# The out-projection as seven block products (Strassen's scheme) instead of eight, in a fused attention and gated-MLP kernel

## The chip, the cores and the metric

The kernel runs on one core of a Trainium2 chip. The metric is the device time of one execution in microseconds; the time of the kernel before is the median of three executions. A profile of one further execution gives the span of the program and what every engine did in it. The engines are called PE (TensorE, matmuls; PEld is its weight load), DVE (VectorE), ACT (ScalarE), POOL (GpSimd) and SP (SyncE, which issues the DMAs).

## The reference

```python
def _attn_ref(q, k, v):                      # q, k, v: 8 x 8 x 576 x 64
    scores = (1 / np.sqrt(D)) * np.matmul(q, k.transpose(0, 1, 3, 2))
    rel = pos[:, None] - pos[None, :]
    mask_local = (rel >= 0) & (rel < 32)                         # heads 0 to 3
    mask_strided = (rel >= 0) & (pos[None, :] % 32 == pos[:, None] % 32)  # heads 4 to 7
    ...
    return np.matmul(softmax(scores), v)

def _moe_ref(x, w_in, w_spatial, b_spatial, w_out):   # x: 8 x 576 x 512
    h = np.maximum(x @ w_in, 0.0)                      # 512 -> 1024
    u, v = h[..., :512], h[..., 512:]
    v_n = (v - mean(v)) / np.sqrt(var(v) + 1e-06)
    v_s = np.einsum('ts,bsd->btd', w_spatial, v_n) + b_spatial[None, :, None]
    gated = u * v_s
    return gated @ w_out                               # 512 -> 512
```

The result of the attention, with its heads side by side, is the x of the second function. All of it is float32.

## The kernel before, in words

The work goes batch by batch (eight batches of 576 positions). Attention makes x in pieces, a pair of heads at a time, two batches ahead of the matrix stages where it can; its matmuls are small. Then each batch has four matrix stages, all on PE:

- `moe_1` computes the v half of h in tiles of 128 positions by 512 columns (L874), which ACT moves out of PSUM with the ReLU and DVE normalises, and the u half transposed, in tiles of 128 features by 288 positions (L916).
- `moe_tail` does the last 64 positions of the normalisation, for one batch (batches 0 and 1) or for two together (the later ones).
- `moe_2` does the spatial matmul for one half of the positions at a time (288 of them; four tiles of 128 features each, L997, L1009, L1010), and DVE multiplies each tile into u (L1019). Then comes the out-projection of that half (`project`, L1039): four tiles of 128 output columns by 288 positions, each a sum over four blocks of 128 features. So the order in a batch is spatial of half 0, project of half 0, spatial of half 1, project of half 1.

PE multiplies float32 numbers in a rounded format here. To keep the accuracy, both operands of every large product are split into a high part (rounded: `rnd`, on ACT, DVE or POOL, L372 and L374) and a remainder (`rest`, a subtraction on DVE, L382), and three products are summed (`PROD`): high by high, high by remainder, remainder by high. A project of one half thus takes 4 tiles x 4 blocks x 3 = 48 matmuls of 288 columns, and a batch takes 96. `gated` is split tile by tile into two buffers of the ring `g`; the weight w_out is split once, at the start, into `w_out_sb` (`weight`, `weights`). ACT copies each finished tile of the output from PSUM to a buffer of the ring `o` (`evac`, L394), and a DMA stores it.

Buffers come from rings: u, g, vv, o and s (PSUM) have two buffers each, vn has one, and the matmul tiles `m` have four PSUM banks. A buffer is written again only when its last reader is done.

No engine chooses at run time. `Program.order()` simulates the program once with a table of priorities (`KEYS`), costs for each engine and latencies, and emits for each engine one fixed sequence; an instruction that waits holds up everything behind it on its engine. The simulation also puts filler matmuls on zeros (L1172) where PE would idle early on; they keep its clock up. `weights` loads each quarter of w_in and w_out (8 bytes a word, packed) into stage buffers of vn, u and g, rebuilds the numbers on ACT, POOL (L758) and DVE (L766), and splits them.

Of the kernel before, what the change touches and what calls it, by code (L numbers as in the profile page):

```python
# [9 lines left out]
F32 = mybir.dt.float32  # L10
F32R = mybir.dt.float32r
# [29 lines left out]
    "a": (-825.9, -1662.1, -696.1, -506.6, 76.7, 35.0, 162.7, 122.5,),  # L41
    "v": (-216.6, -1140.4, -156.0, 19.8,),
    "u": (-158.4, -165.3, 0.3, 367.0,),
    "s": (2476.0, -453.8, 2782.5, 3198.4,),
    "t": (2534.3,),
    "o": (641.4, -137.9, 1268.2, 1486.2,),
    "cst": (-2628.8,),
    "lead": (-0.22,),
    "fill": (170.7, 2011.8, -4312.7, 693.0, -265.9, 735.5,),
    "dp": (844, -15182,),  # L50
    "dpt": (83.09,),
    "lv": (-430.1, -2526.4, -200.5, -140.6,),
    "lu": (-99.7, -488.1, -137.6, -250.6,),
    "lo": (435.1, 82.8, -874.1, 81.6,),
    "ls": (781.6, 39.6, 3113.7, 831.6, 1021.7,),
    "near": (122.22,),
# [6 lines left out]
PROD = ((0, 0), (0, 1), (1, 0))  # L63
FLAT = {2: "p n -> p n", 3: "p a b -> p (a b)", 4: "p a b c -> p (a b c)"}
# [249 lines left out]
def attention_moe(ctx, tc, qT, kT, vl, vs, cst, eye, w_in, w_out, wsp, wtail, out):  # L314
# [14 lines left out]
    w_out_sb = sb.tile([P, 2, NT, DM], F32R, name="w_out_sb")  # L329
# [26 lines left out]
    r_o = Ring(sb, "o", [P, HS], F32, 2)  # L356
# [370 lines left out]

    def weight(key, fetch, src, n, dst, tok, stage):

        buf, i = stage
        if src.dtype == F32:
            val = lambda: buf().bitcast(F32).rearrange(FLAT[len(buf.ring.shape)])[:, 2 * i * n : 2 * i * n + n]
            load(fetch, val, src, [(buf, i, 0), (buf, i, 1)], P * n * 4)
        else:
            raw = lambda dt: buf().bitcast(F32).rearrange(FLAT[len(buf.ring.shape)])[  # L740
                :, 2 * i * n : 2 * (i + 1) * n
            ].bitcast(dt)
            half = lambda j, dt=I32: raw(dt).rearrange("p (n t) -> p n t", t=2)[:, :, j]
            low, top = (buf, i, 0), (buf, i, 1)
            val = lambda dt=F32: half(1, dt)
            load(fetch, lambda: raw(I32), src.bitcast(I32), [low, top], P * n * 8)

            add(
                key, [(ACT, 110 + 0.87 * n)],
                lambda eng: eng.activation(val(), val(), AF.Prelu, scale=2.0**-112, alpha=2.0**32),  # L750
                [], [top],
            )
            def lowest(eng):
                if hasattr(eng, "bn_stats"):
                    eng.tensor_scalar(half(0), half(0), 29, None, op0=ALU.logical_shift_right)
                else:
                    byte = raw(U8).rearrange("p (n t) -> p n t", t=8)[:, :, 3]
                    eng.tensor_scalar(half(0), byte, 1 / 32, -15.5 / 32, op0=ALU.mult, op1=ALU.add)  # L758

            add(  # L760
                key, [(DVE, 70 + 0.52 * n), (POOL, 110 + 1.8 * n)], lowest,
                [], [low], port=(DVE,),
            )
            add(
                key, [(DVE, 70 + 1.04 * n)],
                lambda eng: eng.scalar_tensor_tensor(  # L766
                    half(1), half(1), 3, half(0),
                    op0=ALU.logical_shift_left, op1=ALU.bitwise_or,
                ),
                [low], [top], port=(DVE,),  # L770
            )
# [4 lines left out]
    def weights():  # L776
# [14 lines left out]
        for n, job in enumerate(jobs):  # L791

            def put(job=job, n=n):
                stage = (first, n) if n < NT else ((r_g if n % 2 else r_u).new(), 0)
                weight(*job, stage)
# [457 lines left out]
```

## Time and profile before

| | us |
|---|---|
| median of three executions | 525.32 (524.07, 525.76, 525.32) |
| span of the profiled execution | 521.6 |
| PE busy in that span | 508.8 |
| DVE busy | 332.9 |
| ACT busy | 229.1 |
| POOL busy | 83.6 |

The page gives no time of the profiled execution apart from its span. The 3.7 us by which the median is longer lie around the span, and they are taken to be the same for both kernels.

In the rows of the profile a group reads: line, engine, operation, what it writes <- what it reads, shape, count, then busy time, mean duration in ns, and the idle time of the engine just ahead of these instructions with what ended it. A row of the timeline starts with the start in us and the duration in us; "x6" is that many instructions in a row, and the bracket holds the idle time ahead. A row of the windows gives busy time in us and instructions for PE, PEld, DVE, ACT and POOL, then the granted clock of PE as a share of full speed, the busy share of the DMA engines, and GB/s.

### The profile page before, as it was taken

The numbers are of one execution on the slowest core, as the hardware profiler recorded it, in microseconds if no ns is written. First come the engines' busy times: TensorE is split into PE (matmuls) and PEld (weight loads), VectorE is DVE, ScalarE is ACT, GpSimd is POOL, SyncE is SP. The second block draws the span as 40 slices with busy tenths as digits, with TensorE's granted clock in tenths as the row PEclk, the third lists the DMA queues.
The fourth block names the chain that finished last, engine by engine and source line by source line (L and its number), as shares of the span: only waits on it lengthen the run. The fifth ranks groups of instructions, "written<-read, shape, count | busy, mean of one in ns | idle before, by whom it ended". The sixth has DMA issues, their size and how long they took to land.

```text
span 521.6 us, 14553 instructions
## 1 busy us (share of the span) xinstructions
PE 508.8 (98%) x5980; PEld 468.1 (90%) x5980; DVE 332.9 (64%) x1042; ACT 229.1 (44%) x717; POOL 83.6 (16%) x168
## 2 busy tenths in 40 slices
PE   5899999999999999999999999999999999999997
PEld 3579889889998999989999899998999899998997
DVE  3899996796765758658556667757657553427132
ACT  6688855475534654226432355325432242213111
POOL 2364410233011212002010110202101020001000
PEclk9699999999999999999999999999999999999999
DMA  8788553460333223132243212341111200110011
GB/s 254 253 281 296 203 153 119 132 217 31 102 110 134 78 80 108 41 119 78 80 133 108 70 37 78 133 133 55 43 39 64 87 1 1 47 45 1 1 45 47
DMA packets 26242, 52.65 MB, mean 101 GB/s; under 512 B 3136, under 2 KB 11584, under 8 KB 26176
## 3 DMA queue, kind: packets, MB, share of 16 engines
q1 hardware_dynamic: 26176, 51.72, 30.3%
q8 instruction: 47, 0.77, 0.6%
q14 instruction: 19, 0.16, 0.1%
HBM read 42.27 MB, written 9.44 MB: 99 GB/s over the span
## 4 chain that ended last, share of the span: by engine, by line
PE 88%; DVE 3%; DMA 3%; ACT 3%; SPq 1%; issue 1%; POOL 0%; ACTq 0%; DVEq 0%
PE m L1039 20%; PE m L997 18%; PE m L916 17%; PE m L874 17%; PE po L574 3%; PE po L677 3%; PE s L464 2%; PE s L607 2%; PE m L1009 2%; PE m L1010 2%; DMA g<-w_in 1%; DMA k<-kT 1%; DMA kbd<-kT 1%; PE po L1172 1%; ACT pl L521 1%; SPq L401 1%
## 5 line engine op out<-in xcount | busy, mean ns | idle before, releaser
L997 PE MATMUL m<-wsp_sb,vn 128*128 128x288 f32 x768 | 110.9, 295 | 0.0
L1039 PE MATMUL m<-g,w_out_sb 128*128 128x288 f32 x768 | 107.2, 297 | 0.0
L916 PE MATMUL m<-x,w_in_sb 128*128 128x288 f32 x768 | 106.1, 297 | 0.6 <-DVE w_in_sb L382 0.6
L997 PEld LDWEIGHTS m<-wsp_sb,vn 128*128 128x128 f32 x768 | 105.1, 189 | 0.9
L916 PEld LDWEIGHTS m<-x,w_in_sb 128*128 128x128 f32 x768 | 103.5, 188 | 2.3 <-DVE w_in_sb L382 0.8
L1039 PEld LDWEIGHTS m<-g,w_out_sb 128*128 128x128 f32 x768 | 103.5, 188 | 0.5
L874 PE MATMUL m<-w_in_sb,x 128*128 128x512 f32 (+1 forms) x408 | 99.9, 398 | 0.1
L874 PEld LDWEIGHTS m<-w_in_sb,x 128*128 128x128 f32 (+1 forms) x408 | 74.0, 185 | 19.5 <-DVE w_in_sb L382 0.4
L394 ACT COPY o<-m 128x288 f32<-128x288 f32 x61 | 24.4, 400 | 94.4 <-PE m L1039 82.4
L1019 DVE TENSOR_TENSOR u<-m,u 128x288 f32<-128x288 f32 x64 | 28.0, 451 | 43.5 <-PE m L1010 43.3
L850 POOL TENSOR_TENSOR bn<-bn,sel 128x1 f32<-128x1 f32 (+1 forms) x37 | 21.5, 583 | 182.5 <-DVE bn L845 178.7
L374 POOL TENSOR_SCALAR ptl<-pc 32x64 f32<-32x64 f32 (+3 forms) x74 | 28.8, 390 | 125.0 <-PE po L574 74.9
L521 ACT ACTIVATE pl<-pl,ml 128x64 f32<-128x64 f32 (+1 forms) x140 | 46.9, 338 | 1.8 <-DVE ml L501 1.7
L382 DVE TENSOR_TENSOR x<-po,x 128x288 fp32r<-128x288 f32 x64 | 27.4, 448 | 25.8 <-ACT x L394 25.1
L837 DVE BATCH_NORM_STATS2 bn<-vv 128x6 f32<-128x512 f32 (+1 forms) x37 | 25.4, 690 | 27.5 <-ACT vv L832 27.3
L832 ACT ACTIVATE vv<-m 128x512 f32<-128x512 f32 (+1 forms) x37 | 21.8, 595 | 45.8 <-PE m L874 43.9
L930 ACT ACTIVATE u<-m 128x288 f32<-128x288 f32 x64 | 25.8, 407 | 31.1 <-PE m L916 30.8
L394 ACT CAST x<-po 128x288 fp32r<-128x288 f32 x53 | 20.6, 397 | 42.2 <-PE po L574 29.9
L857 DVE TENSOR_SCALAR vv<-vv,bn 128x512 f32<-128x512 f32 (+1 forms) x37 | 20.6, 555 | 16.8 <-POOL bn L850 16.8
L382 DVE TENSOR_TENSOR g<-u,g 128x288 fp32r<-128x288 f32 x64 | 28.7, 464 | 2.0 <-ACT g L372 0.5
L521 ACT ACTIVATION_READ_ACCUMULATOR pl<-pl,ml 128x1 f32 (+1 forms) x140 | 26.5, 189 | 0.0
L501 DVE CUSTOM_DVE_ANT_0 pl<-s,cst_sb 128x64 f32<-128x64 f32 (+1 forms) x140 | 22.5, 214 | 3.1 <-PE s L464 3.1
(119 smaller groups left out, 564.2 us busy)
## 6 DMA issues: line engine op xcount, KB each, us to landing
q<-qT SPq DMA_DIRECT2D x32, 295.0 KB, 4.1
outT<-o SPq DMA_DIRECT2D x64, 144.0 KB, 1.8
v_raw<-vs SPq DMA_DIRECT2D x15, 512.0 KB, 3.7
v_raw<-vl SPq DMA_DIRECT2D x16, 384.0 KB, 3.6
k<-kT SPq DMA_DIRECT2D x16, 304.0 KB, 4.4
kbd<-kT SPq DMA_DIRECT2D x32, 144.0 KB, 3.5
vn<-w_in SPq DMA_DIRECT2D x4, 512.0 KB, 7.1
u<-w_in SPq DMA_DIRECT2D x3, 512.0 KB, 4.9
```

What stands on the lines that cost most here:

```text
L374: eng.tensor_scalar(dst(), src(), 1.0, 0.0, op0=ALU.mult, op1=ALU.add)
L382: eng.tensor_tensor(dst(), src(), f32(hi()), op=ALU.subtract)
L394: eng.copy(dst(), src())
L501: eng.tensor_tensor_reduce(out=p_sb()[:m, u, :], in0=s_ps[u % 2]()[:m, f0 : f0 + 2 * STRIDE], in1=msk[:m], scale=-SCALE, scalar=3.0e38, op ...
L521: eng.activation(p_sb()[:m, u, :], src, AF.Exp, bias=st()[:m, u : u + 1], scale=SCALE if masked else -1.0, **total,)
L837: lambda eng: eng.bn_stats(bn()[:m, 0:6], v()[:m]), [(v,)], [(bn,)],
L874: eng.matmul(v_ps()[:m, :], x_at(kt)[:, a, :], w_in_sb[:, w, kt, HF:], start=(n == 0 and i == 0), stop=(n == NT - 1 and i == 2),)
L916: eng.matmul(u_ps()[:, :HS], w_in_sb[:, w, kt, f * P : (f + 1) * P], xs[NHP * b + kt]()[:, a, r], start=(n == 0 and i == 0), stop=(n == NT ...
L930: lambda eng, u=u, f=f, u_ps=u_ps: eng.activation(u()[:, f * HS : (f + 1) * HS], u_ps()[:, :HS], AF.Relu),
L997: eng.matmul(s_ps()[:, :HS], vn()[:, a, kt, fs], wsp_sb[:, w, kt, r], start=(kt == 0 and i == 0), stop=False,)
L1019: lambda eng, ug=ug, s_ps=s_ps: eng.tensor_tensor(ug(), s_ps()[:, :HS], ug(), op=ALU.mult),
L1039: eng.matmul(o_ps()[:, :HS], w_out_sb[:, w, f, e * P : (e + 1) * P], g[a]()[:, f, :], start=(f == 0 and i == 0), stop=(f == NT - 1 and i = ...
```

## The change

The out-projection of a batch, 512 features by 512 outputs for 576 positions, is now seen as a 2 x 2 block product: two halves of the features, two halves of the outputs and two halves of the positions. The eight block products are replaced by seven of combined blocks (the form with few additions, due to Winograd). Each block product is 2 output tiles x 2 feature blocks x 3 = 12 matmuls of 288 columns, so a batch takes 84 instead of 96, and the program 672 instead of 768.

What is added:

- Weights: `w_out_sb` holds seven blocks (three of w_out and four combinations s1 to s4). `weight_blocks` makes the four combinations for each of two feature blocks by adds and subtractions of 256 columns on DVE (L784, 8 in all) and splits 14 blocks of 256 columns, where there were 4 of 512.
- Gated: after both halves of the spatial matmul DVE makes t1 to t4 by eight adds and subtractions of 288 columns a batch (L784), and the pieces b11, b21, t1, t2, t3, t4, b22 are split: 14 roundings and 14 remainders a batch, where there were 8 of each. b11, b21, t4 and b22 lie in the ring g, t1, t2 and t3 in the one buffer of vn, which the spatial matmul of that batch has just read; t2 unsplit lies in o.
- Sums: two tiles alpha get a11 x b11; ACT copies that (L398) into vv (`snap`), and a12 x b21 goes on top: that is the output of one block. The rest is summed by ten additions a batch on DVE (`plus`, L1155), each of a PSUM tile and a buffer in SBUF, where four of the eight copies out of PSUM were. The stores leave from o and, two a batch, from vv.

Moved or set anew: `moe_2` does the spatial matmul of both halves first and the seven products after; the ring o has four buffers; `dynamic_dma_scratch_size` is 1024; the table KEYS has other numbers throughout, and a planning cost of stage 2 is 24.4 instead of 25.6. So the order of everything else on all engines differs as well. By the emitted program, the roundings of gated pieces were on DVE (36) and ACT (28), and are now on ACT (86) and POOL (26); DVE has no copies from PSUM and no roundings of vn any more.

The core of the diff (helpers that only rearrange what `weight` did are left out):

```diff
+BLOCKS = ("a11", "a12", "a22", "s1", "s2", "s3", "s4")
...
-    r_o = Ring(sb, "o", [P, HS], F32, 2)
+    r_o = Ring(sb, "o", [P, HS], F32, 4)
...
+    def combine(key, n, dst, in0, in1, op, reads, writes):
+        add(
+            key, [(DVE, 70 + 1.04 * n), (POOL, 120 + 2.3 * n)],
+            lambda eng: eng.tensor_tensor(dst(), in0(), in1(), op=op), reads, writes,
+            port=(DVE, POOL),
+        )
...
-        spatial(0, key)
-        project(0, key + 6.9)
-        spatial(1, key + 12.8)
-        project(1, key + 19.7)
+        spatial(0, key)
+        spatial(1, key + KEYS["p"][0])
...
+        side = r_vn.new()
+        ring = {name: r_g.new() for name in ("b11", "b21")}
+        t2 = [r_o.new() for _ in range(2)]
...
+        def plus(key, o_ps, src, src_buf, dst, dst_buf):
+            add(
+                key, [(DVE, 70 + 1.04 * HS)],
+                lambda eng: eng.tensor_tensor(dst(), o_ps()[:, :HS], src(), op=ALU.add),
+                [(o_ps,), (src_buf,)], [(dst_buf,)],
+            )
...
+        for a in range(2):
+            product("a11", "b11", alpha[a], a, at_step(), True)
+            evac(k0 + KEYS["p"][2] * a, HS, snap(a), lambda a=a: alpha[a]()[:, :HS], [(alpha[a],)], [(s1[a],)])
+        for a in range(2):
+            product("a12", "b21", alpha[a], a, t, False)
...
+        for a in range(2):
+            product("s2", "t2", beta[a], a, t, True)
+            plus(t, beta[a], snap(a), s1[a], r1[a], r1[a])
+        for a in range(2):
+            product("s1", "t1", gamma[a], a, at_step(), True)
+            product("s3", "t3", beta[a], a, t, False)
+            plus(t, beta[a], snap(a), s1[a], r2[a], r2[a])
+            plus(t + 0.2, gamma[a], r2[a], r2[a], r2[a], r2[a])
+        for a in range(2):
+            product("a22", "t4", beta[a], a, t, False)
+            plus(t, beta[a], snap(a), s1[a], snap(a), s1[a])
+            product("s4", "b22", gamma[a], a, t, False)
+            plus(t, gamma[a], r1[a], r1[a], r1[a], r1[a])
...
-    cost = {1: 22.3, 0: 2.6, 2: 25.6}
+    cost = {1: 22.3, 0: 2.6, 2: 24.4}
```

Where the order moved, in three places. First PE, at the end of the last batch: what follows the last spatial tile. Before (the project of half 1, 48 matmuls; m_7006 and m_7019 are PSUM tiles, g_6958 and g_6963 the high parts and the remainders):

```order
L1010 MATMUL m_6988<-wt_b,tail_b_75 128x288
L1039 MATMUL m_7006<-g_6958,w_out_sb 128x288
L1039 MATMUL m_7006<-g_6963,w_out_sb 128x288
L1039 MATMUL m_7006<-g_6958,w_out_sb 128x288 x2
L1039 MATMUL m_7006<-g_6963,w_out_sb 128x288
```

After (m_7080 and m_7091 are alpha, m_7116 and m_7135 beta, m_7144 and m_7164 gamma, each for output tile 0 and 1; g_6957 is b11, g_6994 is b21, and vn_7077 holds t1, t2 and t3):

```order
L1127 MATMUL m_7080<-g_6957,w_out_sb 128x288 x6
L1127 MATMUL m_7091<-g_6957,w_out_sb 128x288 x6
L1127 MATMUL m_7080<-g_6994,w_out_sb 128x288 x6
L1127 MATMUL m_7116<-vn_7077,w_out_sb 128x288 x3
L1127 MATMUL m_7091<-g_6994,w_out_sb 128x288 x6
L1127 MATMUL m_7135<-vn_7077,w_out_sb 128x288 x3
L1127 MATMUL m_7144<-vn_7077,w_out_sb 128x288 x3
L1127 MATMUL m_7116<-vn_7077,w_out_sb 128x288 x3
L1127 MATMUL m_7135<-vn_7077,w_out_sb 128x288 x3
L1127 MATMUL m_7144<-vn_7077,w_out_sb 128x288 x3
L1127 MATMUL m_7164<-vn_7077,w_out_sb 128x288 x3
L1127 MATMUL m_7116<-vn_7077,w_out_sb 128x288 x6
```

The 84 matmuls of the batch now stand behind all its spatial tiles; the one that writes m_7116 again (the last row, s3 x t3) may start only when `plus` has read that bank.

Second DVE, at the same place: what it does between the last spatial tile and the end. Before, three instructions for each tile (multiply, round, remainder; u_6757 is half 1 of u), of which the last two tiles:

```order
L1019 TENSOR_TENSOR u_6757<-m_6970,u_6757 128x288
L374 TENSOR_SCALAR g_6958<-u_6757 128x288
L382 TENSOR_TENSOR g_6963<-u_6757,g_6958 128x288
L1019 TENSOR_TENSOR u_6757<-m_6988,u_6757 128x288
L374 TENSOR_SCALAR g_6958<-u_6757 128x288
L382 TENSOR_TENSOR g_6963<-u_6757,g_6958 128x288
```

After (u_6832 and u_6894 are the two halves of u, o_7065 and o_7101 are t2 for the two feature blocks, g_7107 is t4, g_7141 is b22):

```order
L1060 TENSOR_TENSOR u_6894<-m_7057,u_6894 128x288
L386 TENSOR_TENSOR vn_7077<-o_7065,vn_7077 128x288
L386 TENSOR_TENSOR vn_7077<-u_6894,vn_7077 128x288
L784 TENSOR_TENSOR o_7101<-u_6894,u_6832 128x288
L784 TENSOR_TENSOR u_6894<-u_6894 128x288
L386 TENSOR_TENSOR vn_7077<-u_6832,vn_7077 128x288 x2
L784 TENSOR_TENSOR u_6832<-u_6832,o_7101 128x288
L386 TENSOR_TENSOR g_7107<-u_6832,g_7107 128x288
L386 TENSOR_TENSOR vn_7077<-o_7101,vn_7077 128x288
L386 TENSOR_TENSOR vn_7077<-u_6894,vn_7077 128x288
L386 TENSOR_TENSOR g_7107<-u_6832,g_7107 128x288
L386 TENSOR_TENSOR g_7141<-u_6894,g_7141 128x288 x2
```

Behind the last multiply there are now thirteen instructions with both inputs in SBUF ahead of the first `plus`, where there were two instructions; three of the roundings that they wait for (t2 and t3 for the second feature block, and one of b22) stand on POOL.

Third SP, at the start of the program: the order of the loads. Before:

```order
L1089 DMA cst_sb<-cst 128x192
L401 DMA o_89<-eye 128x128
L401 DMA vn_93<-w_in 128x1024
L401 DMA q_101<-qT 128x590
L401 DMA k_107<-kT 128x608
```

After:

```order
L405 DMA vn_84<-w_in 128x1024
L1225 DMA cst_sb<-cst 128x192
L405 DMA o_92<-eye 128x128
L405 DMA u_96<-w_in 128x1024
L405 DMA q_104<-qT 128x590
L405 DMA k_111<-kT 128x608
```

Two pieces of w_in, rather than one, are now ahead of the first q and k. On PE, the filler matmuls behind the first scores are seven rows (fourteen passes) instead of four (eight passes).

294 lines of the change are left out of this document (194 added, 100 removed).

## The prediction

> **What bounds it now.** I read the page first: its busy times, the slices of the span and the chain that ended last.
>
> ```profile
> span 521.6 us, 14553 instructions
> PE 508.8 (98%) x5980; PEld 468.1 (90%) x5980; DVE 332.9 (64%) x1042; ACT 229.1 (44%) x717; POOL 83.6 (16%) x168
> PE   5899999999999999999999999999999999999997
> DVE  3899996796765758658556667757657553427132
> PEclk9699999999999999999999999999999999999999
> PE 88%; DVE 3%; DMA 3%; ACT 3%; SPq 1%; issue 1%; POOL 0%; ACTq 0%; DVEq 0%
> ```
>
> PE is busy in 98% of the span, at full clock after the second slice, and makes up 88% of the chain. DVE is the second engine. It is full only in slices 3 to 6, about 26 to 78 us, when the weights are split beside attention. Then I cut the span into windows: start, middle and end.
>
> ```profile
> 13.00:26.00 13.00, 10.58 (x194) 7.06 (x195) 11.42 (x31) 8.74 (x28) 4.48 (x12) 0.68 0.76 251
> 26.00:39.00 13.00, 12.55 (x105) 9.19 (x105) 12.71 (x25) 10.53 (x21) 7.83 (x10) 1.00 0.87 281
> 52.00:78.00 26.00, 25.46 (x457) 23.13 (x456) 25.05 (x77) 18.21 (x58) 8.80 (x16) 1.00 0.56 179
> 234.00:286.00 52.00, 52.00 (x702) 49.99 (x701) 34.00 (x119) 23.31 (x82) 6.42 (x16) 1.00 0.29 97
> ```
>
> In the middle PE has no gap in 52 us, with DVE at 34.00 of 52 and POOL at 6.42. So from about 23 us on the time is the number of PE slots, and at the start it is what lets PE begin. The chain of waits gives the price of a slot, and the groups that of the vector work.
>
> ```profile
> 511.84 6.41 PE m L1039 x48
> L382 DVE TENSOR_TENSOR g<-u,g 128x288 fp32r<-128x288 f32 x64 | 28.7, 464 | 2.0 <-ACT g L372 0.5
> L1019 DVE TENSOR_TENSOR u<-m,u 128x288 f32<-128x288 f32 x64 | 28.0, 451 | 43.5 <-PE m L1010 43.3
> L374 DVE TENSOR_SCALAR g<-u 128x288 fp32r<-128x288 f32 x36 | 11.1, 309 | 1.2
> L372 ACT CAST g<-u 128x288 fp32r<-128x288 f32 x28 | 11.2, 432 | 17.0 <-DVE u L1019 17.0
> L394 ACT COPY o<-m 128x288 f32<-128x288 f32 x61 | 24.4, 400 | 94.4 <-PE m L1039 82.4 <-DMA outT<-o 9.3 <-PE po L574 2.2
> ```
>
> Forty-eight matmuls follow each other in 6.41 us: 0.1335 us each (the 297 ns of a matmul's own record are latency). One piece takes 0.46 us of DVE for a two-input operation, 0.43 us of ACT for a rounding, 0.40 us for a copy.
>
> **Matmuls removed.** 96 slots at 0.1335 us: **-12.8 us**. All of them lie on PE where it has no gap, so the whole sum counts as far as PE stays fed. That six matmuls now go to one PSUM tile and the next six to another costs nothing that I can see: the 48 of the row above changed tile too, on the way.
>
> **Vector work added.** A batch gets 8 combinations, 6 remainders and 10 additions more on DVE, 24 at 0.46 = 11.0 us, and loses 4.5 roundings at 0.31 = 1.4 us, and 12 roundings of vn in the whole program: some 9 us a batch, 72 us in all, so DVE goes from 333 to about 405 of 515 us, 79%. ACT gets 58 roundings at 0.43 (25 us) and loses 29 copies at 0.40 (12 us). Neither engine becomes the bound on average. The cost can only come from the place where PE waits for them, and that is the end of each batch, where the products now stand together. The trace of before has the same wait in a milder form:
>
> ```profile
> 340.58 0.46 DVE L1019 TENSOR_TENSOR u<-m,u 128x288 f32<-128x288 f32 x1 [0.56 <-PE m L1010]
> 341.07 0.31 DVE L374 TENSOR_SCALAR g<-u 128x288 fp32r<-128x288 f32 x1
> 341.42 0.46 DVE L382 TENSOR_TENSOR g<-u,g 128x288 fp32r<-128x288 f32 x1
> 68.09 1.55 DVE L382 TENSOR_TENSOR g<-u,g 128x288 fp32r<-128x288 f32 x4
> ```
>
> Operations that wait for each other start 0.49 us apart (340.58, 341.07), and four independent ones take 1.55 us, 0.37 each from start to start. I walked through the last batch with these, t = 0 being the start of a11 x b11 on PE. PE needs 12 slots each (1.60 us) for a11 and a12 and for s2 and s1, which are interleaved; s3 x t3 wants to start at 24 + 21 slots, t = 6.0. It writes a beta bank that the first `plus` must have read. That `plus` stands behind the last multiply and thirteen two-input operations on DVE: one 0.49, and thirteen between 0.37 and 0.49 by what they depend on, which makes 5.5, then itself 0.46: it ends at t = 5.96 if no rounding is late. So on DVE's own speed it just fits, and this place costs nothing. The pieces before are no tighter: b11 and b21 come from half 0, long split; t2 and t1 for block 0 have 2.4 us of a11 and a12 in front of them.
>
> Three of the roundings stand on POOL. The timeline of before shows what happens to POOL when DVE is busy:
>
> ```profile
> 38.69 0.66 POOL L758 TENSOR_SCALAR u<-u 128x512 int32<-128x512 uint8 x1 [2.56 <-ACT vv L832]
> 59.68 1.69 POOL L758 TENSOR_SCALAR g<-g 128x512 int32<-128x512 uint8 x1
> 59.42 0.72 DVE L382 TENSOR_TENSOR w_out_sb<-g,w_out_sb 128x512 fp32r<-128x512 f32 x1
> 60.06 0.74 DVE L382 TENSOR_TENSOR wsp_sb<-x,wsp_sb 128x576 fp32r<-128x576 f32 x1
> 235.90 0.49 POOL L374 TENSOR_SCALAR pts<-pc 32x288 f32<-32x288 f32 x1 [1.89 <-PE po L677]
> ```
>
> The same POOL operation took 0.66 us alone and 1.69 us while DVE ran two subtractions with both inputs in SBUF, and it ended (61.37) only after the second of them (60.80). I read that as POOL standing still during such operations. A rounding of 288 columns is 0.49 us on POOL, by its row on fewer partitions. In the new place DVE runs nothing but such operations, so POOL gets in only where DVE waits for another reason, and then DVE waits for POOL. In the walk the rounding of t2 for block 1, ready at t = 1.8, runs from 3.44 to 3.93, and that of b22 costs DVE another half. The first `plus` then ends at 6.36 to 6.82 rather than 5.96: **0.8 us of PE** by the upper end, which I take as both delays fall ahead of it. Bounds: 0 (POOL finds gaps) and 1.9 (all three roundings in series with DVE, 3 x 0.95, less 0.95 of slack).
>
> The Trainium skill, "SBUF — State Buffer", section "Who interferes with whom", says that a DVE instruction with two SBUF inputs contends with a GpSimd instruction that reads SBUF, and that whichever issues first holds the shared ports for its whole length. The 1.69 us row agrees with it. By that rule the new `plus`, with one input in PSUM, would not hold POOL, and the sum would be the one given here; without it the term of 0.8 would be nothing.
>
> By the emitted orders the same pattern stands in batches 2, 4, 6 and 7 (0.8 each). In 0 and 1 other work of DVE gives POOL gaps, and I take 0.3 each; in 3 and 5 attention's matmuls stand between the products on PE and cover it. Sum 4 x 0.8 + 2 x 0.3 = **+3.8 us**, bounds 0 and 15 (8 x 1.9).
>
> **Buffers.** Half 1 of spatial no longer waits for a project in between, and g is freed twice a batch; vn is held for t1 to t3 until s3 x t3 (t = 8), and the next batch's vn is needed only when its first v tile is normalised, at t = 11.2 + 2.8 = 14.0. The vv buffers are held by alpha until their store lands, about t = 12 to 13.3; the ReLU of the next v tile needs one at 14.0. If a store took longer, ACT's ReLU would be seen waiting for the output's DMA, and PE behind it. In before ACT waited 9.3 us for stores of o, off PE's path; four o buffers remove that and gain nothing. The smaller DMA scratch moves no instruction.
>
> **The start.** The rows there:
>
> ```profile
> 2.58 0.43 SPq L401 DMA_DIRECT2D k<-kT  x1
> 8.38 0.96 PE L464 MATMUL m<-k,q 64*32 64x64 f32 x72 [1.71 <-DMA k<-kT]
> 16.36 3.61 PE L1172 MATMUL po<-zeros 128*32 128x256 f32 x8
> 16.29 2.17 POOL L374 TENSOR_SCALAR ptl<-pc 32x320 f32<-32x320 f32 x5 [9.19 <-DVE pc L545]
> 19.90 1.83 PE L574 MATMUL po<-ptl,v_raw 128*64 128x96 f32 x24
> 22.75 1.67 PE L874 MATMUL m<-w_in_sb,x 128*128 128x512 f32 x6
> vn<-w_in SPq DMA_DIRECT2D x4, 512.0 KB, 7.1
> ```
>
> PE waits for k until 8.38 us. One more piece of w_in, 512 KB, now goes ahead; at the 251 GB/s of the window from 13 to 26 us that is **+2.0 us** for q, k and all behind them. Six more filler passes at 3.61/8 = 0.45 stand ahead of the first weighted values: up to 2.7 us more if they end the wait, nothing if the prepared weights (ptl, ready at 16.29 + 2.17 = 18.5, then 20.5) end it. I take nothing, since fillers at a granted clock near 1 would go twice as fast, and the 0.68 of the window from 13 to 26 shows it rising there. Against that, an early second piece of w_in may save some of PE's idle time later (0.45 us from 26 to 39, 0.54 from 52 to 78, at most some 1 us net of the delay). The 14 weight blocks and 8 combinations of 256 columns are some 10 operations more on a DVE that has no gap there (12.71 of 13.00), but roundings left it; counted by the emitted orders at the durations of such rows, its work ahead of the first gated multiply is 39.8 us instead of about 39.2. So +2.0, bounds -1 and +4.7.
>
> **The end.** The last store now waits for a `plus` of 0.46 us on DVE rather than for a copy of 0.40 on ACT: **+0.1**.
>
> Sum: the profiled span 521.6 - 12.8 + 2.0 + 3.8 + 0.1 = 514.7, and with the 3.7 us that lie around it **518.4 us**, to be compared with the median 525.3.
>
> **Rivals.**
> 1. *Everything hidden.* POOL's roundings find their gaps and the fillers and loads cost nothing: 525.3 - 12.8 = 512.5, between 509 and 514.5. For it: DVE has 34 of 52 us in the middle, and the walk fits without POOL's stalls. Against it: k does come later. Chance 0.20.
> 2. *A long start and stalls in every batch.* Start +4.7 and 0.7 in each of the eight batches (5.6): 525.3 - 12.8 + 4.7 + 5.6 = 522.8, between 521 and 526. For it: the filler row of 3.61 us, and DVE as late in batches 3 and 5 as elsewhere. Against it: these have small matmuls on PE between the products. Chance 0.20, a third of it above 523.7.
> 3. *Slower: POOL and DVE hold each other up.* The mechanism is the one of the 1.69 us row, at the place between the last multiply and the first `plus`, at 1.9 us a batch: 525.3 - 12.8 + 2.0 + 8 x 1.9 = 529.7. It decides from (12.8 - 2.0)/8 = 1.35 us a batch. Against it: ACT does most of the roundings, and of a batch's fourteen only about three are POOL's. Chance 0.08.
> 4. *It does not do what it says.* The products could cost as much as before if changing tiles and waiting for the bank after every three or six matmuls spoilt the 0.1335 us of a slot, by a seventh: about 525. Nothing in the trace speaks for it. Chance 0.04.
>
> **How the numbers follow.** My forecast's own band, 514.5 to 521, has 0.48. The range from 510.5 to 524.5 leaves out the lower tail of rival 1, the upper of rival 2, and rivals 3 and 4, together just under 2 in 10. A measurement here can tell about 0.3% or 1.6 us from no change. Faster, below 523.7: 0.48 + 0.20 + two thirds of rival 2 = 0.82; within, 0.10; slower, 0.08.
>
> **What would show it.** In the profile after: 672 out-projection matmuls, and each 12 of them in 1.60 us; PE's waits for `plus` (its beta bank) of about 0.8 us in batches 2, 4, 6 and 7; POOL roundings of t2 well over 0.5 us; PE's first scores near 10.4 us instead of 8.38, and the first v tile near 24.5 instead of 22.75. A PE wait for vv, vn or a store would show a buffer that I took as hidden; first scores at 8.4 or a first tile above 27 would make the start wrong.

## The result, and the profile after

The changed kernel takes 522.06 us (median of four executions, 521.19 to 523.10) against 524.91 for the kernel before in the same comparison: a ratio of 0.995, with a 95% interval from 0.9936 to 0.9965. It is faster, inside the range of the prediction, but by 2.9 us rather than the 6.9 that were forecast. The profiled execution has a span of 519.2 us instead of 521.6, 2.4 less. In every execution that has both numbers on record the time is about 2.0 us above the span (here 521.19 and 519.2). By that reckoning the profiled execution of before took about 523.6 us, and of the 3.7 us that were put around the span ahead some 1.7 are the spread from one execution to the next; the sum of the prediction is not changed by this, since it carries the 3.7 on both sides.

The page of the changed kernel, its first rows and the head of the chain that ended last:

```profile
span 519.2 us, 14653 instructions
PE 502.4 (97%) x5892; PEld 457.8 (88%) x5892; DVE 366.9 (71%) x1101; ACT 264.3 (51%) x809; POOL 125.0 (24%) x253
PE   7889899999999999999999999999999999999997
DVE  2899999888597847967389655986469651776166
PEclk9799999999999999999999999999999999999999
PE 71%; DVE 18%; ACT 4%; DMA 2%; POOL 2%; issue 2%; SPq 1%; DVEq 0%; POOLq 0%; ACTq 0%
```

DVE is now 18% of the chain; it was 3%. Its busy time rose by 34 us, not by the 72 that I had counted from durations: the profile counts a stretch once where instructions overlap, and with the new order DVE makes no roundings for attention either (ACT rose by 35 us, POOL by 41). The row of PE has eights in slices 3 and 5, where there were nines. The same windows as before:

```profile
13.00:26.00 13.00, 10.43 (x201) 6.67 (x198) 10.88 (x26) 9.97 (x33) 6.61 (x15) 0.77 0.95 323
26.00:39.00 13.00, 10.71 (x148) 7.87 (x152) 12.09 (x22) 8.94 (x19) 8.70 (x11) 1.00 0.82 294
52.00:78.00 26.00, 23.83 (x230) 21.84 (x229) 25.09 (x55) 15.76 (x48) 13.46 (x23) 0.93 0.40 138
234.00:286.00 52.00, 51.40 (x763) 48.42 (x764) 37.35 (x122) 29.74 (x98) 11.62 (x26) 1.00 0.27 85
```

In the middle PE is idle for 0.6 of 52 us. From 26 to 39 it is idle for 2.3 us (0.45 before), from 52 to 78 for 2.2 (0.54 before), and there the granted clock is 0.93. So more time per microsecond is lost at the start than in the middle. The longest of PE's waits in the changed kernel (us in all, times, longest):

```profile
PE m L611 <- DMA kbd<-kT: 2.4, 1, 2.4
PE m L1038 <- DVE wsp_sb L386: 1.6, 1, 1.6
PE m L468 <- DMA k<-kT: 1.4, 1, 1.4
PE s L468 <- DMA k<-kT: 1.4, 1, 1.4
PE m L1127 <- DVE vn L386: 1.4, 3, 0.6
PE po L681 <- POOL pts L378: 1.1, 1, 1.1
PE po L681 <- DVE mx L421: 1.0, 1, 1.0
PE m L1308 <- DVE sel L1242: 0.9, 1, 0.9
PE m L1127 <- DVE o L1155: 0.6, 4, 0.2
PE m L1050 <- DVE tail L386: 0.6, 1, 0.6
```

L1038 and L1050 are the spatial matmuls, L1127 the products, L1155 `plus`. To see how much each stage lost, I took three marks from the starts of PE's rows: the first v tile of batch 0, the first v tile of batch 1 and the last matmul. PE does the same attention work between the marks in both kernels.

```profile
93.81 1.57 PE L874 MATMUL m<-w_in_sb,x 128*128 128x512 f32 x6
```

That is before; after it is these two rows:

```profile
22.95 1.84 PE L916 MATMUL m<-w_in_sb,x 128*128 128x512 f32 x6
98.14 1.57 PE L916 MATMUL m<-w_in_sb,x 128*128 128x512 f32 x6
```

| us | before | after | difference | by the slots alone | lost |
|---|---|---|---|---|---|
| start to first v tile | 22.75 | 22.95 | +0.2 | 0 | 0.2 |
| first v tile to batch 1 | 71.06 | 75.19 | +4.1 | -1.6 | **5.7** |
| batch 1 to the last matmul (517.94; 515.53) | 424.13 | 417.39 | -6.7 | -11.2 | **4.5** |
| last matmul to the end of the span | 3.66 | 3.67 | 0.0 | 0 | 0.0 |

The sum, -2.4, is the difference of the spans. "By the slots alone" is the number of slots times 0.1335 us. The first mark moves by a microsecond or two from one profile to the next (22.95 to 25.72 in twelve profiles with this load order; 22.75 and 23.74 in the two with the order before), so in what follows I compare the second row, called **the start** below, and the third, **the rest**.

In the start PE waits for DVE, and then its clock falls (timeline of the changed kernel, PE from 61 us):

```profile
61.33 0.40 PE L1038 MATMUL m<-wsp_sb,vn 128*128 128x288 f32 x1
63.29 7.21 PE L1038 MATMUL m<-wsp_sb,vn 128*128 128x288 f32 x41 [1.55 <-DVE wsp_sb L386]
71.11 0.40 PE L1050 MATMUL m<-wt_h,tail 128*128 128x288 f32 x1 [0.62 <-DVE tail L386]
```

And two windows of it, with the granted clock in the third column from the right:

```profile
63.00:65.00 2.00, 1.71 (x7) 1.72 (x8) 2.00 (x5) 0.00 (x0) 0.00 (x0) 0.61 0.83 246
65.00:67.00 2.00, 2.00 (x10) 2.00 (x10) 2.00 (x7) 0.70 (x1) 0.89 (x2) 0.53 1.09 363
```

PE waited 1.55 us for a remainder of w_spatial, and then ran at half clock for 3.4 us, ten matmuls in 2 us instead of fifteen. Then it waited again, for the tail of the normalisation. Which of these costs time is what the first experiments ask.

In the products, each wait looks small, since the rows of PE overlap; the delay shows from start to start (batch 7, then batch 3):

```profile
507.65 2.56 PE L1127 MATMUL m<-vn,w_out_sb 128*128 128x288 f32 x18
510.37 2.27 PE L1127 MATMUL m<-vn,w_out_sb 128*128 128x288 f32 x15 [0.16 <-DVE o L1155]
...
276.92 1.49 PE L1127 MATMUL m<-vn,w_out_sb 128*128 128x288 f32 x10
279.02 1.72 PE L1127 MATMUL m<-vn,w_out_sb 128*128 128x288 f32 x11 [0.60 <-DVE vn L386]
```

Eighteen slots from 507.65 end at 510.05, and the next matmul starts at 510.37: 0.32 late, with another 0.1 on its successor. In batch 3 ten slots from 276.92 end at 278.26, and the next starts at 279.02, 0.76 late. Reckoned in this way batches 2, 4, 6 and 7 have the first delay, batch 5 has that of batch 3 (0.74), and batch 1 has one of 0.34.

### The profile page after: what moved, and what is told of

Read it like the earlier page. It is cut to its first block, busy times and chain, and to the rows that moved or that the text cites. A ratio compares the mean times of both kernels' runs of the same rounds, so it can differ in the third digit from the quotient of the medians.

```text
span 519.2 us, 14653 instructions
## 1 busy us (share of the span) xinstructions
PE 502.4 (97%) x5892; PEld 457.8 (88%) x5892; DVE 366.9 (71%) x1101; ACT 264.3 (51%) x809; POOL 125.0 (24%) x253
## 4 chain that ended last, share of the span: by engine, by line
PE 71%; DVE 18%; ACT 4%; DMA 2%; POOL 2%; issue 2%; SPq 1%; DVEq 0%; POOLq 0%; ACTq 0%
PE m L958 18%; PE m L916 16%; PE m L1038 14%; PE m L1127 10%; DVE vn L386 3%; PE po L681 3%; PE po L578 3%; PE s L468 2%; DVE u L784 2%; PE s L611 1%; DVE g L386 1%; DVE u L1060 1%; PE m L1050 1%; PE m L1051 1%; DMA k<-kT 1%
## 5 line engine op out<-in xcount | busy, mean ns | idle before, releaser
L1038 PE MATMUL m<-wsp_sb,vn 128*128 128x288 f32 x768 | 113.5, 299 | 1.6 <-DVE wsp_sb L386 1.6
L1038 PEld LDWEIGHTS m<-wsp_sb,vn 128*128 128x128 f32 x768 | 106.8, 191 | 2.5 <-DVE wsp_sb L386 1.8
L378 POOL TENSOR_SCALAR ptl<-pc 32x320 f32<-32x320 f32 (+3 forms) x104 | 40.3, 388 | 90.1 <-ACT x L398 32.3
L1127 PE MATMUL m<-g,w_out_sb 128*128 128x288 f32 x384 | 56.8, 299 | 0.2 <-ACT vv L398 0.2
L1127 PEld LDWEIGHTS m<-g,w_out_sb 128*128 128x128 f32 x384 | 52.6, 188 | 1.1 <-ACT vv L398 0.4
L1127 PE MATMUL m<-vn,w_out_sb 128*128 128x288 f32 x288 | 44.0, 300 | 2.1 <-DVE vn L386 1.4
L1127 PEld LDWEIGHTS m<-vn,w_out_sb 128*128 128x128 f32 x288 | 39.6, 188 | 4.3 <-DVE vn L386 2.2
L398 ACT CAST x<-po 128x288 fp32r<-128x288 f32 x64 | 24.7, 398 | 36.0 <-PE po L578 24.3
L376 ACT CAST g<-u 128x288 fp32r<-128x288 f32 x54 | 22.4, 432 | 27.1 <-DVE u L1060 20.6
L376 ACT COPY ptl<-pc 32x320 f32<-32x320 f32 (+3 forms) x88 | 31.4, 357 | 5.9 <-DVE pc L549 4.0
L899 DVE TENSOR_SCALAR vv<-vv,bn 128x512 f32<-128x512 f32 (+1 forms) x37 | 20.6, 557 | 19.3 <-POOL bn L892 19.1
```

Source lines behind the costliest of these rows:

```text
L376: eng.copy(dst(), src())
L378: eng.tensor_scalar(dst(), src(), 1.0, 0.0, op0=ALU.mult, op1=ALU.add)
L398: eng.copy(dst(), src())
L1038: eng.matmul(s_ps()[:, :HS], vn()[:, a, kt, fs], wsp_sb[:, w, kt, r], start=(kt == 0 and i == 0), stop=False,)
L1127: eng.matmul(o_ps()[:, :HS], w_out_sb[:, b_at, w, kk, a * P : (a + 1) * P], at(j, kk), start=first and kk == 0 and i == 0, stop=kk == 1 an ...
```

## The experiments

Except for the first, all are the changed kernel with one edit to the emitted order: the order is computed as it is, and then some instructions are put on another engine, moved behind others on their engines, or left out. `delay(held, until)` moves the instructions `held`, and what depends on them, behind `until`; `tag` only names instructions.

### The slots alone

```diff
                         for i, (w, a) in enumerate(PROD):
+                            if i == 2 and (f == 1 or (f == 2 and e < 2)):
+                                continue
                             eng.matmul(
```

> The kernel before with 12 of the 96 out-projection matmuls of a batch left out (the products of the weight's remainder with one and a half of the four feature blocks), in the same order on every engine and with all vector work. It prices the slots alone. Theory (a slot is 0.1335 us and PE has no gap behind the first tile): 96 x 0.1335 = 12.8 us less than before, 512.1 against 524.9. Rival (the vector engines or the transfers set part of the time and would take a share back): 515 or more.

Measured: 512.11 us (before 524.19; ratio 0.9769, 0.9755 to 0.9784). The rest took 413.42 us, 10.7 less than before. So 96 slots are worth 12.1 us here, and this term holds. The start took 70.47 us, only 0.6 less than before and not 1.6: with fewer slots ahead of it PE comes to the gated pieces of half 1 of batch 0 before they are split, and waits there. Against this run, and not against counted slots, the changed kernel loses 4.7 us in the start and 4.0 in the rest.

### Is the fall of the clock what costs?

Four rows of fillers ahead of the first spatial matmul:

```diff
+        first = next(n for _, n, e in issued if self.tags.get(n) == ("spatial",))
+        self.extra[first] = 4
```

> The changed kernel with four rows of filler matmuls (1.7 us of PE) put ahead of the first spatial matmul of batch 0, where PE then waits 1.55 us for a remainder of w_spatial. Nothing else moves. Theory (the idle time made the granted clock fall to half for 3.4 us): the wait shrinks below 0.5 us, the clock stays at 1.00 from 63 to 67 us, the spatial matmuls there follow each other in 0.13 us instead of 0.24, and about 1.7 us are gained: 520.4. Rival (those matmuls are slow because transfers at 246 to 363 GB/s run in the same stretch, or since their operands come late): they stay at 0.24 us, 522. Second rival (the split weights of w_out are late as well): the stage is faster but the first products wait, gain under 0.5 us.

Measured: 522.77 us (ratio 0.9977, 0.9962 to 0.9991). PE in the same stretch:

```profile
64.99 5.67 PE L1081 MATMUL m<-wsp_sb,vn 128*128 128x288 f32 x41 [0.50 <-DVE wsp_sb L419]
72.67 0.40 PE L1096 MATMUL m<-wt_h,tail 128*128 128x288 f32 x1 [2.02 <-DVE tail L419]
```

And the windows of it:

```profile
65.00:67.00 2.00, 2.00 (x15) 2.00 (x16) 2.00 (x4) 0.00 (x0) 0.00 (x0) 1.00 0.91 309
67.00:69.00 2.00, 2.00 (x17) 2.00 (x16) 2.00 (x9) 0.69 (x1) 1.22 (x2) 1.00 0.98 338
```

The mechanism is as I thought: with the hole filled the clock stayed at 1.00, and the matmuls ran at full pace beside transfers at 309 to 338 GB/s, so these were not the cause. But nothing was gained. The matmuls were done sooner, and PE waited 2.02 us rather than 0.62 for the tail. My price for it was wrong: the fall of the clock lies beside DVE's work. The second rival had the gain right, but the wait that I wrote down for it stood at the products, and it came at the tail.

### Does the order on DVE cost?

First, of w_out's work only what stands between the remainders of w_spatial is moved:

```diff
+        held = {n for k, v in named.items() if k[-1] == "w_out" for n in v}
...
+        issued = issued[:start] + self.delay(issued[start:], held, [n for n in rests if order.index(n) >= start])
```

> The changed kernel with the combinations, roundings and remainders of w_out that stand between the remainders of w_spatial on DVE and POOL moved behind the last of these; nothing else moves. Theory (PE's wait of 1.55 us at the first spatial matmul is DVE's queue: w_out's work stands ahead of what PE needs): the wait is below 0.3 us, the clock doesn't fall, and 1.5 + 1.7 = 3.2 us are gained: 518.9. Rival (w_out's second half, which loads into the buffers that the first half leaves, then comes late): the first products of batch 0 wait 2 us or more, and the time is 521 or more.

Then all of it, behind the tail of batch 0:

```diff
+        held = {n for k, v in named.items() if k[-1] == "w_out" for n in v}
+        issued = self.delay(issued, held, named["tail",])
```

> The changed kernel with all work on w_out's blocks that stood ahead of the remainder of the tail of batch 0 moved behind it; nothing else moves. Theory (the sum of DVE's work ahead of the first products is the bound, in whatever order): the tail is ready 3 to 5 us earlier, the spatial stage ends earlier, and the products wait that much longer for w_out; 521 to 524. Rival (only its place ahead of the tail costs): the products don't wait, 518 to 519.

Measured: 524.89 (ratio 1.0007, 0.9993 to 1.002) and 527.39 (1.0065, 1.0042 to 1.0088). With w_spatial first PE had no wait there, and then waited 5.53 us for the tail. The theory's 518.9 was wrong; the rival had the time right (521 or more), but put the wait at the products. The tail came 1.8 us later after the first tile than in the changed kernel, and DVE had stood 1.23 us for POOL ahead of it. With w_out behind the tail, the tail was ready 4.8 us earlier in relation to the first tile, but then came this, on DVE and PE:

```profile
76.27 0.69 DVE L798 SCALAR_TENSOR_TENSOR g<-g 128x512 int32<-128x512 int32 x1 [3.53 <-POOL g L790]
76.87 0.25 DVE L458 RECIPROCAL mx<-mx 128x16 f32<-128x16 f32 x1
77.04 0.40 DVE L1108 TENSOR_TENSOR u<-m,u 128x288 f32<-128x288 f32 x1
...
77.49 3.25 PE L1083 MATMUL m<-wsp_sb,vn 128*128 128x288 f32 x12 [7.40 <-DVE u L1108]
```

The second pair of w_out's pieces is loaded into the buffers that the first pair leaves. Split later, the first pair left them later, and DVE stood 3.53 us at an instruction that waited for that load, with the gated multiplies behind it; PE waited 7.40 us for these. So w_out is a chain of two rounds through two buffers, and moving it back only makes it longer. The first part of my theory held (an earlier tail, no gain); the price was too small, as I had not thought of the load.

### How much of the start is DVE's work on w_out?

The remainders left out, the combinations left out, and both edits together:

```diff
+        dropped = {n for k, v in named.items() if k[0] == "rest" and k[-1] == "w_out" for n in v}
+        issued = [i for i in issued if i[1] not in dropped]
...
+    nc.gpsimd.memset(f32(w_out_sb[:, :, 1].rearrange("p b k n -> p b (k n)")), 0.0)
```

> The changed kernel without the 14 remainders of w_out's blocks: that half of the split weight is set to zero once at the start, so the products of the weight's remainder count nothing in the output. The matmuls and the order stay. It takes 14 x 0.43 = 6 us of DVE out of the time ahead of the first products, 3.1 of it ahead of the normalised tail. Theory (DVE is the bound from about 26 us to the first products, and the work that the change adds there is what the start lost): the first tile of batch 1 starts 3 to 6 us earlier in relation to the first tile of batch 0, and the time is 517 to 519. Rival (loads, POOL and the split of w_in set the start, DVE only fills the time): under 1 us, 521 or more.

```diff
+        dropped = set(named["combine", "w_out"])
+        issued = [i for i in issued if i[1] not in dropped]
```

> The changed kernel without the eight combinations of w_out (its blocks s1 to s4 then hold what stood in their buffers, and the products of these blocks are not the reference's). It takes 4.4 us of DVE out, 2.3 of it ahead of the tail of batch 0. Theory (the start's loss is DVE's work on w_out, given back at the rate that leaving out the remainders showed, 3.6 us for 6.0): batch 1 starts 2 to 3.5 us earlier after the first tile than in the changed kernel (75.19 us there), and the time is 519 to 520.5. Rival (only the remainders are on the path, since PE waits for these): under 1 us, 521 or more.

> The changed kernel without the eight combinations and without the 14 remainders of w_out (that half of the split weight is zero): neither is in the output. 10.4 us of DVE less, the matmuls as in the changed kernel. Theory (all of the start's loss is DVE's work on w_out): from the first tile to batch 1 it takes 69 to 71 us, where the kernel before took 71.06 with 12 slots more, and the time is 515.5 to 517.5. Rival (a second part of the loss lies in loads, POOL and attention): 72.5 us or more, 518 or more.

The price of this work in the changed kernel, in three groups:

```profile
L386 DVE TENSOR_TENSOR w_out_sb<-g,w_out_sb 128x256 fp32r<-128x256 f32 x14 | 6.0, 462 | 0.0
L784 DVE TENSOR_TENSOR g<-g,g 128x256 f32<-128x256 f32 x4 | 2.3, 585 | 0.0
L784 DVE TENSOR_TENSOR g<-g 128x256 f32<-128x256 f32 x4 | 2.1, 528 | 0.0
```

| left out | DVE | the start | given back | time | ratio (95%) |
|---|---|---|---|---|---|
| nothing | | 75.19 | | 522.06 | 0.995 (0.9936 to 0.9965) |
| 8 combinations | 4.4 | 73.46 | 1.7 | 520.92 | 0.9933 (0.9919 to 0.9947) |
| 14 remainders | 6.0 | 71.57 | 3.6 | 519.16 | 0.9910 (0.9885 to 0.9935) |
| both | 10.4 | 70.51 | 4.7 | 517.99 | 0.9885 (0.9869 to 0.9901) |

The start gives back 0.4 to 0.6 of each microsecond that DVE is spared, and 4.7 us with all of it gone. Three edits that leave DVE's work on w_out as it is (fill, nopool, t4only) have starts of 75.48 to 75.64, so differences of a few tenths mean nothing here. Its length was as expected for norest and noboth; for the combinations alone it was a little less (1.7 for "2 to 3.5"), and the times of norest, nocomb and noboth came out 0.2, 0.4 and 0.5 us above what I had written.

Not all of the 10.4 us is the change's doing: the kernel before has four remainders of w_out too, of 512 columns and 0.69 us each, 2.8 us. At the rate above, leaving those out would give back 1.1 to 1.7 us. So by estimate the work that the change adds on DVE accounts for 3.0 to 3.6 us, the larger part of the 4.7 to 5.7 us lost. The remainder is not attributed; the next experiment finds a part that comes from POOL.

### POOL

```diff
+        moved = {n for k, v in named.items() if k[0] == "rnd" and k[-1] == "w_out" for n in v}
+        issued = [(at, n, ACT if e == POOL and n in moved else e) for at, n, e in issued]
```

> The changed kernel with the eight roundings of w_out that stand on POOL put on ACT in the same places. Theory (POOL's roundings stretch DVE's two-input operations there: a combination of 256 columns took 0.64 to 0.89 us beside them and 0.41 otherwise): the tail of batch 0 is ready about 1 us earlier, 521. Rival (ACT is as full there, its roundings come late and DVE waits for them): 522 to 523.

```diff
+        gated = {n for k, v in named.items() if k[0] == "rnd" and k[1] in ("b11", "b21", "t1", "t2", "t3", "t4", "b22") for n in v}
+        issued = [(at, n, ACT if e == POOL and n in gated else e) for at, n, e in issued]
```

> The changed kernel with the 26 roundings of gated pieces that stand on POOL put on ACT at the same places; the order is otherwise the same. Theory of the prediction (POOL and DVE hold each other up): the first addition of a batch ends 0.3 to 0.5 us earlier, PE's waits of 0.3 to 0.8 us at s3 x t3 vanish in batches 2 to 7, and some 3 us are gained: 519. Rival (it is the length of DVE's own queue between the last multiply and that addition, thirteen or more operations at 0.37 us): the waits stay within 0.15 us of what they were, 521.5 to 522.5.

Measured: 520.69 (ratio 0.994, 0.9917 to 0.9963) and 521.17 (0.9946, 0.9932 to 0.996). Their intervals overlap that of the changed kernel, so by time alone neither is told from it. The trace shows more. Of the first, three groups of DVE from 54 to 82 us:

```profile
L419 DVE TENSOR_TENSOR w_out_sb<-g,w_out_sb 128x256 fp32r<-128x256 f32 x14 | 5.3, 415 | 0.0
L821 DVE TENSOR_TENSOR g<-g,g 128x256 f32<-128x256 f32 x4 | 1.7, 416 | 0.0
L821 DVE TENSOR_TENSOR g<-g 128x256 f32<-128x256 f32 x4 | 1.7, 415 | 0.0
```

Without POOL's roundings beside them a combination takes 0.42 us rather than 0.53 to 0.59, and the start is 0.9 us shorter (74.30). Of the second, batch 7 of the changed kernel shows what it changes (POOL, then DVE):

```profile
505.89 0.58 POOL L378 TENSOR_SCALAR vn<-o 128x288 fp32r<-128x288 f32 x1 [1.36 <-DVE o L784]
507.97 0.57 POOL L378 TENSOR_SCALAR g<-u 128x288 fp32r<-128x288 f32 x1 [1.50 <-ACT g L376]
...
508.76 1.18 DVE L386 TENSOR_TENSOR g<-u,g 128x288 fp32r<-128x288 f32 x3
509.87 0.81 DVE L1155 TENSOR_TENSOR o<-m,vv 128x288 f32<-128x288 f32 x2
```

POOL is not kept out while DVE is busy: its rounding of t2 starts 0.09 us after its input is ready (505.80) and takes 0.58 us, where the one at 504.10 took 0.43. But two roundings like this stretch DVE's queue, and the first `plus` ends 6.3 us after a11 x b11 began (504.04); in nopool it is 6.0, the moment at which PE wants the bank. PE's wait for `plus` is gone in all batches, as the theory of the prediction has it, but the rest is only 0.8 us shorter (416.6 against 417.4), and the 519 that I had written was too low. The 0.8 is what is left of a larger gain: ACT, with those roundings ahead of its copies, now keeps PE waiting for alpha, by start to start 0.2 to 0.4 us in batches 1, 2, 4, 6 and 7 and twice 0.3 in batches 3 and 5. The list of PE's waits in nopool has only some of it:

```profile
PE m L1173 <- ACT vv L431: 0.7, 4, 0.2
```

### The place of the first additions

```diff
+        for b in range(8):
+            held = {n for k, v in named.items() if k[0] == "rest" and k[1:2] in (("b22",), ("t4",)) and k[-1] == b for n in v}
+            issued = self.delay(issued, held, named["plus", b])
```

> The changed kernel with the first two additions of each batch put ahead of the remainders of t4 and b22 on DVE; POOL keeps its roundings. Theory (the wait at s3 x t3 is the length of DVE's queue ahead of that addition): PE's waits for it, 0.3 to 0.45 us in batches 2, 4, 6 and 7, vanish, 520.5. Rival (POOL's rounding of t2 holds the queue up ahead of those remainders already): the waits stay above half, 521.5 to 522.5.

Measured: 519.79 (ratio 0.9898, 0.9876 to 0.992), apart from the changed kernel's interval; the rest is 2.4 us shorter (414.96). DVE in batch 7:

```profile
507.27 0.44 DVE L420 TENSOR_TENSOR vn<-u,vn 128x288 fp32r<-128x288 f32 x1
508.52 0.86 DVE L1202 TENSOR_TENSOR o<-m,vv 128x288 f32<-128x288 f32 x2 [0.80 <-PE m L1174]
509.29 1.55 DVE L420 TENSOR_TENSOR g<-u,g 128x288 fp32r<-128x288 f32 x4
...
507.12 4.56 PE L1174 MATMUL m<-vn,w_out_sb 128*128 128x288 f32 x33
```

With POOL as it was, the additions (L1202 here) now wait 0.80 us for PE instead of PE for them, and PE runs its 33 matmuls without a gap. So the wait in batches 2, 4, 6 and 7 has two causes that are both needed: a queue on DVE ahead of the additions that just fits, with four remainders in it that PE needs only later (1.5 us), and POOL's roundings, which make it too long. Taking either away removes this wait, but only this edit does it without a new one. In batches 3 and 5, 0.37 of the 0.76 us stays.

### The order of the loads

```diff
+        loads = [n for _, n, e in issued if e == DMA]
+        issued = self.delay(issued, {loads[3]}, [loads[8]])
```

> The changed kernel with the second piece of w_in loaded behind the second k instead of ahead of the first q; nothing else moves. The prediction's term: the first scores start 1.2 us earlier, everything behind them too, and about 1 to 2 us are gained: 520 to 521. Rival (the start is bound later, by DVE's work, and an early second piece feeds that): the first scores start earlier, but the tail of batch 0 and batch 1 do not, 522 or more.

Measured: 525.02 (ratio 1.0007, 0.9991 to 1.0022), 3 us slower than the changed kernel. The first scores did start earlier, but DVE then stood at the piece of w_in:

```profile
8.55 0.96 PE L501 MATMUL m<-k,q 64*32 64x64 f32 x72 [0.78 <-DMA k<-kT]
...
12.91 0.69 DVE L798 SCALAR_TENSOR_TENSOR u<-u 128x512 int32<-128x512 int32 x1 [4.86 <-POOL u L790]
14.32 0.69 DVE L419 TENSOR_TENSOR w_in_sb<-u,w_in_sb 128x512 fp32r<-128x512 f32 x1 [0.71 <-ACT w_in_sb L409]
14.93 0.88 DVE L521 TENSOR_REDUCE ml<-m 128x5 f32<-128x320 f32 x2
```

The scores were 1.0 us earlier (9.57 before this edit), and the softmax, which stands behind w_in's instruction on DVE, began 4.2 us later (14.93 instead of 10.71). The first v tile came at 26.17 us. With the order of DVE and POOL as the change has it, the early load pays; an order made for the late load wasn't tried.

### Together

mix1 has the two edits on POOL and that of t4only. mix2 is mix1, but the roundings of gated pieces in batches 3 and 5 stay on POOL, and in these two batches the lines below are added to t4only's loop; mix3 is mix2 with the edit of kfirst.

```diff
+            if b in (3, 5):
+                issued = self.delay(issued, held | set(named["t4", b]), named["rest", "t3", 1, b] + named["rest", "t2", 1, b])
```

> The changed kernel with no rounding of gated pieces or of w_out on POOL (all on ACT), and with the first two additions of each batch put ahead of the remainders of t4 and b22 on DVE. Theory (the waits at s3 x t3 come from POOL and from the remainders that stand ahead of the first addition): PE has no wait over 0.15 us for an addition in any batch, and the time is 519 to 520.5. Rival (what is left is the start, and the waits only move to the later pieces): 521 or more.

> As mix1 (no rounding of w_out or gated pieces on POOL, first additions ahead of the remainders of t4 and b22), but in batches 3 and 5 POOL keeps its roundings, and t4's combinations go behind the remainders of t2 and t3. Theory (in those two batches ACT, given POOL's roundings, was late with the copies of alpha, 0.87 us a batch): waits in batches 3 and 5 below 0.4 us, 519.0. Rival (DVE's queue is too long there in any order): 0.8 us stay, 519.8 or more.

> mix2 with the load order of kfirst. Theory of the prediction (a late k costs 1 us or more): 518.0. Rival (DVE's work bounds the start): as mix2 or slower, 519 or more.

Measured: 519.77 (ratio 0.9919, 0.9895 to 0.9942), **519.05** (0.9892, 0.9869 to 0.9914) and 522.46 (0.9948, 0.9927 to 0.9968). mix1 and mix2 came out as expected, mix3 as its rival. mix2 beats both the kernel before and the change; its lead on t4only, 0.7 us, is inside the intervals. It has no wait for a product left in its list of PE's waits, but by start to start its products are still 0.2 to 0.3 us late for alpha in batches 2, 4, 6 and 7: its rest, 415.6 us, is longer than the 414.96 of t4only, and its lead lies in the start (74.03 against 75.64). t4only with w_out's roundings alone moved off POOL wasn't tried. mix1 shows that batches 3 and 5 lose some 0.86 us, as in nopool, when ACT is given POOL's roundings, and mix3 that the late load costs about the same here too (3.4 us).

## Why the prediction was only half right

- **The slots, -12.8 us.** Right: leaving them out alone gave -12.1.
- **The start, +2.0 us.** This is the step that failed, in its size and in its cause. It was made of a later k, and of DVE's work on the new weights it took next to nothing: "39.8 us instead of about 39.2" ahead of the first gated multiply. A later k is there (first scores at 9.57 instead of 8.38 us). How much of it reaches the first v tile the profiles don't settle: it came 0.2 us later in the profile after, and in the twelve profiles with this load order its median is 24.1. Undoing the load order made the kernel slower. What was lost is 4.7 to 5.7 us behind the first tile, and leaving out DVE's work on w_out gives back 4.7, by estimate 3.0 to 3.6 of them work that the change adds. The count went wrong in two ways. From the first v tile to the first gated multiply DVE was busy for 46.8 us where it was 41.7 before, 5.1 more and not 0.6; a part of that is that instructions are longer beside POOL (the combinations took 0.53 to 0.59 us and 0.42 without POOL's roundings). And it stopped at the first multiply, though four combinations and seven remainders more, 4.5 us by their rows, stand between that multiply and the first product. I had the row that says that DVE is full there, 12.71 of 13.00, and costed an edit beside it at nearly nothing.
- **The products, +3.8 us.** About the right size (4.5 us from batch 1 on, or 4.0 against the run of the slots alone), partly by luck. The walk through DVE's queue was right: it "just fits", and without POOL's roundings the first `plus` ends at 6.0 (nopool) where I had 5.96. That POOL's roundings make it late was right as well, at 6.3 rather than the 6.36 to 6.82 of the walk. But the way was wrong: POOL did not have to wait for DVE to be idle, and its rounding of t2 began at 1.85 on that clock and not at 3.44. The sizes by place were wrong too and made up for each other: 0.32 us and its echo in batches 2, 4, 6 and 7 rather than 0.8, and 0.76 in batches 3 and 5, where I had nothing, since I let attention's matmuls cover them; DVE's own attention work stands in the same queue. And I overlooked the cheaper cure: shortening the queue gave 2.4 us back with POOL left alone, and taking POOL's roundings away 0.8.
- **The rule that was weighed** (the Trainium skill, "SBUF — State Buffer", section "Who interferes with whom"): the trace agrees that two-input operations of DVE and POOL's roundings stretch each other (combinations of 0.53 to 0.59 against 0.42 us; POOL's roundings of w_out took 0.62 us on average, 0.42 at the least). The rule was right about the stretch; I made too much of it when I let POOL stand still for as long as DVE has such work.
- **Buffers.** Right: no product waited for a ring buffer. ACT waited 4.2 us in two places for the stores from vv, which PE does not show. **The end**, +0.1, was 0.0. The DMA scratch and the four buffers of o weren't tried by themselves.
- **The rivals.** What happened is nearest to the second, a long start with stalls in most batches, 522.8; it had a chance of 0.20. Its time fits better than its cause: its longer start came from loads and fillers, and the one that the runs show from DVE.

## What to carry to other kernels

An algorithm that saves matmuls pays with vector work, and this must be counted where it stands, not as an average: DVE had a third of its time free here, and hardly any of it where the new weights had to be made (in the kernel before it is busy for 41.7 of the 43.75 us from the first v tile to the first gated multiply). Look in an in-order queue for what stands ahead of the instruction that the bound engine waits for, and move what is needed later behind it: four remainders moved back gave 2.3 us here. A gap on the bound engine, even one that makes its clock fall, was worth nothing to close here, because the next thing that it needed came later still.

## What was not expected of the hardware

- A wait of PE of 1.55 us, behind 1.9 us of small attention matmuls, was enough for the granted clock to fall to 0.5, for 3.4 us; with four rows of fillers in it, and 0.50 us idle left, it did not fall. In wspfirst, where PE waited 5.53 us, it was at 0.5 for 6.8 us.
- In twelve profiles with the same load order the clock rose to full between 19.1 and 22.1 us, and the first v tile came between 22.95 and 25.72. A difference of a microsecond in the span of a single profile says little; differences between marks within it say more, down to a few tenths.
